# A hand-planned two-layer attention and MLP kernel: one row block's statistics moved to ScalarE, W2 loaded in two parts, and planner ranks set per step

## The chip, the cores and the metric

The kernel runs on one core of one Trainium2 chip. Its time is the device time of one execution in microseconds (us), as a median over several runs. A core has five engines with their own instruction streams: PE (TensorE, matmuls), DVE (VectorE), ACT (ScalarE), POOL (GpSimd) and SP (SyncE, which here only issues DMA transfers). PE reads SBUF and writes PSUM; ACT and DVE carry results from PSUM back to SBUF.

## The reference: two layers, each of windowed attention and an MLP

The input x has 2048 rows of 512 numbers in bf16. Weights are Wqkv (512 x 1536), Wo (512 x 512), W1 (512 x 1792) and W2 (1792 x 512), shared by both layers.

```python
for _ in range(2):
    x = x + attention(layernorm(x), wqkv, wo)   # 32 heads of 16, causal, window of 256 keys
    x = x + relu(layernorm(x) @ w1) @ w2
# attention: p = softmax(mask(q @ k.T * 16**-0.5)); o = p @ v; return concat(o) @ wo
# layernorm: (x - mean(x)) / sqrt(var(x) + 1e-5), no gain, no bias
```

## The kernel before: a planner writes each engine's order

The rows are cut into four chunks of 512. A step k is one chunk in one layer, so there are eight steps, 0 to 3 for the first layer and 4 to 7 for the second. In each step the work is:

- `plan_qkv(k)`: for each row block j of 128 rows (four in a chunk), statistics (`norm_stats`: `bn_stats` and `bn_aggr` on DVE, epsilon added for two blocks at once), the power -1/2 on POOL (`norm_pow`, for two blocks at once), the normalized bf16 block `xn` (`norm_apply`), and its transpose `xnT`. Step 0 transposes on PE with a copy out of PSUM, all others by a DMA transpose issued from SP. Then K, Q and V matmuls; `spread_k` writes K into the block-diagonal tile `KBD`, `spread_v` writes V into `V2f`.
- `plan_attention(k)`: scores, exp, masks and probabilities times V. Heads are handled in four tiles t of eight heads. A *score group* is a set of short matmuls `Sps<-Qt,KBD` into the one PSUM buffer `Sps` (four banks), followed by one exp on ACT (`Pb<-Sps`, up to 2048 elements per partition), followed by masks on `Pb` (`affine_select` on POOL or a minimum on DVE). There are 156 score groups, in a fixed order; group s may only start when the exp of group s-1 has read `Sps`. Below they are called S0 to S155, and the stretch from one to the next a *slot*. Then `acc<-V2f,Pb` (2880 matmuls of 34 columns, called pv below), a reciprocal and a multiply (`divide`) give O.
- `plan_rest(k)`: O is transposed (`OT<-O`, a DMA transpose from SP for each of the four row blocks, three buffers; on PE in the last step), multiplied by Wo, added to x; then the second layernorm (`xn`, `xn2T` again by DMA transposes), W1 with relu (`hT`, 14 groups of 4 matmuls) and W2 (4 groups of 14).

No order is written by hand. At build time each of these pieces is an `Op` with a key (its rank), the engines that may run it with a duration for each, and what it depends on. A list scheduler walks through time: when an engine is free it takes the ready Op with the lowest rank (on PE the key alone; on the others the ready time plus the key). The order that comes out is fixed in each engine's stream, so on the chip each engine runs its list in order and waits at each entry until its inputs are there. The ranks are `SOON` (for the copies out of PSUM, masks, divisions and additions), `calm` (statistics of early steps), `wait` (how many score groups ahead of its first use a K/Q group ranks, 16), the pace of V groups (1.6), and `d0`, `d1` (the stretch of score groups over which W1 and W2 are spread). `act_free` lets ACT take another piece ahead of the next exp only if that piece ends, by the planner's times, at most 0.1 us after the score group that is running, or 0.55 us after a coming one could start. When the planner sees PE idle for 0.4 us it inserts a matmul `warm<-ident` whose result nobody reads. Scores have the lowest key, so they go first; W1 and W2 fill what is left.

W2 is loaded by one DMA from SP, ranked after the transposes of step 1's `xnT`.

Of the kernel before, what the change touches and what calls it, by code (L numbers as in the profile page):

```python
# [15 lines left out]
P = 128  # L16
# [23 lines left out]
PW = 576  # L40
SHOW = None
# [29 lines left out]
def kernel(  # L71
# [122 lines left out]
    SOON = {'qkv': -0.5, 'v': 0, 'h': -1, 'mask': -1, 'div': 0, 'add': -2}  # L194
    LINK = {"PE": 0.2, "DVE": 0.2, "ACT": 0.2, "POOL": 0.2, "SP": 0.2}
# [64 lines left out]
    EVAC = {512: {"DVE": 0.67, "ACT": 0.59}, 256: {"DVE": 0.42, "ACT": 0.38}}  # L260
# [21 lines left out]
    def norm_stats(lid, j, src, deps, eps_from=None, key=0):  # L282
        def fn():
            st = small.tile([P, 6], FP32, name="st", bufs=4)
            dve.bn_stats(out=st[:], in_=src)
            dve.bn_aggr(out=mvs[:, lid % 8, j, :], in_=st[:])
            if eps_from is not None:
                dve.tensor_scalar_add(rstds[:, lid % 8, eps_from:j + 1], mvs[:, lid % 8, eps_from:j + 1, 1], 1e-5)
        return op(key, {"DVE": (0.86 + (0.18 if eps_from is not None else 0), fn)}, deps)

    def norm_pow(lid, j0, j1, deps, key=0):
        r = rstds[:, lid % 8, j0:j1]
        return op(key, {"POOL": (0.72, lambda: pool.tensor_tensor(out=r, in0=r, in1=mhalf[:, j0:j1], op=ALU.pow))}, deps)

    def norm_apply(lid, j, src, deps, by_array, dst, then_key, dst_deps):

        box = Box(xns)
        mv, r, nb = mvs[:, lid % 8, j, :], rstds[:, lid % 8, j:j + 1], nbs[:, lid % 8, j:j + 1]

        def fn(e):  # L300
            box.t = box.tile([P, D], BF16, "xn")
            if e == "DVE":
                dve.tensor_scalar(out=box.t[:], in0=src, scalar1=mv[:, 0:1], scalar2=r, op0=ALU.subtract, op1=ALU.mult)
            else:
                pool.tensor_tensor(out=nb, in0=mv[:, 0:1], in1=r, op=ALU.mult)
                pool.tensor_scalar(out=nb, in0=nb, scalar1=-1.0, scalar2=None, op0=ALU.mult)
                pool.tensor_scalar(out=box.t[:], in0=src, scalar1=r, scalar2=nb, op0=ALU.mult, op1=ALU.add)
        times = {"DVE": 0.52} if by_array else {"POOL": 1.4, "DVE": 0.54}
        a = op(-10 if lid == 0 else 0, options(times, fn), list(deps) + list(dst_deps), box)
        if by_array:  # L310
            return transpose(then_key, lambda: box.t[:], lambda: dst[0][:, :, j * P:(j + 1) * P], [a], [box])

        def dma():
            sp.dma_start_transpose(out=dst[0][:, :, j * P:(j + 1) * P],
                                   in_=box.t[:].rearrange("p (kc d) -> p kc d", kc=KC))
        return op(0, {"SP": (1.22, dma, 2.6)}, [a], None, [box])

    def transpose(key, src, dst, deps, uses, take=None):
        box = Box(psum)

        def fn():
            box.ps = box.tile([P, KC, P], BF16, "tp")
            for kc in range(KC):
                pe.transpose(box.ps[:, kc, :], src()[:, kc * P:(kc + 1) * P], ident[:])
        t = op(key, {"PE": (0.26, fn)}, deps, box, list(uses) + [box])
        return op(0, options({"DVE": 0.42, "ACT": 0.59}, lambda e: copy(e, dst(), box.ps[:])), [t], take, [box])
# [121 lines left out]
    c_tri = [op(3, {"POOL": (0.55, lambda i=i: triangle(i))}, [c_tri0]) for i in range(3)]  # L448
# [5 lines left out]
    c_v = [op(-2, {"DVE": (0.4, lambda e=e: v_ones(e))}, c_v0) for e in range(2)]  # L454
# [16 lines left out]
    def plan_qkv(k):  # L471
# [5 lines left out]
        calm = (-10, 1, 40, 60)[k] if k < 4 else 0  # L477
        for j in range(4):
            came = [d_x[j // 2] if c == 0 else d_xc[c]] if layer == 0 else [x_done[k - 4, j]]
            st.append(norm_stats(lid, j, src[j], came + applied.get(lid - 8, []), j - 1 if j % 2 else None, calm))  # L480
# [14 lines left out]
        wait = 0 if k == 0 else 16  # L495
        for h in range(2) if k == 0 else (None,):
# [5 lines left out]
            for t in range(4):  # L502
# [7 lines left out]
                k_done[k, t, h or 0] = op(SOON["qkv"], options(times, lambda e, t=t, h0=h0, h1=h1, box=box:  # L510
# [12 lines left out]
                q_done[k, t, h or 0] = op(SOON["qkv"], options(EVAC[w], qev), [m2], None, [box])  # L523
                mine += [m, m2]
        for j in range(4):
            at = first_slot[units_of[k][0]] + (1 + (8 if j > 1 else 0) if k == 0 else 1.6 * j - wait)
# [9 lines left out]
            ev = op(SOON["qkv"], options(EVAC[512], vev), [m], vs, [box, vs])  # L536
            v_done[k, j] = op(SOON["v"], options({"POOL": 1.72, "DVE": 1.42} if k else {"POOL": 1.72, "DVE": 1.42, "ACT": 1.48}, lambda e, j=j, vs=vs: spread_v(e, layer, c, j, vs.t[:])),
# [3 lines left out]
    def plan_attention(k):  # L541
        layer, c = divmod(k, NCH)
        prev = units_of.get(k - 1, []) if c else []
        for n in units_of[k]:
# [3 lines left out]
            for g in range(len(u.groups)):  # L548
# [17 lines left out]
                for m in u.masks(g):  # L566
                    times = {"DVE": 0.32 + 0.14 * (len(m) - 1), "POOL": 0.93 * len(m)}
                    masks[s].append(op(SOON["mask"], options(times, lambda e, m=m, g=g, pb=pb: mask(e, m, places(pb, g))), [exps[s]] + c_tri))
            for j0 in range(0, u.nq // 2, 2):
# [23 lines left out]
                def dfn(u=u, j=j, box=box):  # L593
# [4 lines left out]
                    SOON["div"], {"DVE": (0.64, dfn)}, [prior] + war + checks[k - 2:k - 1], None, [box])  # L598
# [3 lines left out]
    def plan_rest(k):  # L602
# [12 lines left out]
        for j in range(4):  # L615
# [6 lines left out]
            if final:  # L622
                t = transpose(-20000 + k, lambda j=j: O_of[k][:, j, :], to, ready, [ob], ob)
            else:
                t = op(-5, {"SP": (1.22, lambda j=j, to=to: sp.dma_start_transpose(
                    out=to(), in_=O_of[k][:, j, :].rearrange("p (kc d) -> p kc d", kc=KC)), 2.6)}, ready, ob, [ob])
# [8 lines left out]
            add = op(SOON["add"], {"DVE": (0.68, lambda j=j, box=box: residual(4 * c + j, box.ps[:], layer == 0))}, [m], None, [box])  # L635
# [11 lines left out]
        for j0, j1 in ((0, 2), (2, 4)) if k in HALVED else ((0, 4),):  # L647
            if k in HALVED:
                d0 = first_slot[units_of[k][3 + 2 * j0]] + 8
                d1 = d0 + 10  # L650
            else:
                d0, d1 = base[k + 1] + 7, base[k + 1] + 24
            n0, n1 = P * j0, P * j1
            evs = []
            for f in range(NF):
# [10 lines left out]
                evs.append(op(SOON["h"], options(EVAC[n1 - n0], hev), [m], None, [box]))  # L666
            for j in range(j0, j1):
                for n0, n1 in ((0, 256), (256, 512)) if final and j == 3 else ((0, 512),):
# [14 lines left out]
                    else:  # L683
                        x_done[k, j] = op(SOON["add"], {"DVE": (0.68, lambda j=j, box=box: residual(4 * c + j, box.ps[:], False))},
# [3 lines left out]
    for k in range(NSTEP):  # L688
        plan_attention(k)
        if k == 0:  # L690
            plan_qkv(1)
            d_w2 = op(0, {"SP": (1.4, lambda: sp.dma_start(w2[:], B_w2.rearrange("(f p) n -> p f n", p=P)), 9.0)}, applied[2])
        plan_rest(k)
        if 0 < k < NSTEP - 1:
            plan_qkv(k + 1)
# [50 lines left out]
    def act_free(t, us):  # L746
# [4 lines left out]
        if scores[s].number in started:  # L751
            return t + us <= score_end[0] + 0.1
        return t + us <= max(t, scores[s].at("PE")) + 0.55
# [22 lines left out]
    while events and events[0][0] < 3000:  # L776
# [16 lines left out]
        for e in ENGINES:  # L793
# [7 lines left out]
            elif e == "PE" and done_ops[0] < len(ops) - 12:  # L801
                if t - idle_since[0] >= (0.4 if t > 20 else 0.0) and sum(1 for f, _ in psum.free if f <= t) > 1:
# [167 lines left out]
```

## Time and profile before

| | |
|---|---|
| time, median of 9 runs | 481.33 us (480.7 to 483.81) |
| the profiled execution, own time | 482.59 us |
| its span, first to last instruction | 480.9 us |
| mean granted TensorE clock | 0.998 |
| busy: PE, DVE, ACT, POOL | 461.3, 356.1, 336.6, 300.0 us |
| `warm` matmuls | 40 |
| exps on ACT (`Pb<-Sps`), all forms | 156, 282.6 us, 1812 ns each |
| `OT<-O`, `xnT<-xn`, `xn2T<-xn` DMA transposes | 28 each, 2.5 us median from issue to landing |
| W1 and W2 loads | 1792 KB each, 11.1 us median to landing |

Busy time of PE is the union of matmul intervals, each counted from issue to the end of its pipeline; a busy PE can still be losing time. A row of the timeline gives the start, the length, the engine, the source line, the instruction, what it writes and reads, how many were merged, and in brackets how long the engine was idle before it and what ended that wait. All instructions of the step pieces go through one recording helper and so carry its line, L114; tiles are told apart by name. SPq rows are the issues of DMA transfers.

### The profile page before, as it was taken

Reading aid. Unit: us, or ns where it says so; the run is one execution under the profiler, and the core shown is the slowest. Engines: PE = TensorE matmul, PEld = TensorE weight load, DVE = VectorE, ACT = ScalarE, POOL = GpSimd, SP = SyncE. Lnnn points to the kernel's source line nnn. Section 1 sums busy time; section 2 is a strip of 40 time slices with the busy share of each in tenths; the row PEclk is TensorE's granted clock in tenths of the full one; section 3 lists DMA queues with packets and bytes.
Section 4 is the critical chain, followed back from the end, with each engine's and each line's share of the span. In section 5 each row is a group of like instructions: output and inputs, shape, how many; then the busy total and the mean of one; then the engine's idle time right before and its main releaser. Section 6 shows DMA issues by size and latency. Waiting matters only on the chain.

```text
span 480.9 us, 14303 instructions
## 1 busy us (share of the span) xinstructions
PE 461.3 (96%) x5967; PEld 244.3 (51%) x5967; DVE 356.1 (74%) x852; ACT 336.6 (70%) x263; POOL 300.0 (62%) x665
## 2 busy tenths in 40 slices
PE   7999999998999989999999999999999999999994
PEld 3555646654555535555544555544555545464443
DVE  6999988867987589977999887897559876464101
ACT  3878777877777668877778876777768777644330
POOL 7788868546776788846975766685766657421000
PEclk9999999999999999999999999999999999999999
DMA  8770321004200052002411023010331103000101
GB/s 266 254 204 3 68 23 25 2 3 67 57 12 3 2 90 45 4 1 45 68 24 36 12 34 57 12 35 2 56 68 25 34 1 68 25 1 11 34 12 38
DMA packets 54792, 21.96 MB, mean 46 GB/s; under 512 B 46145, under 2 KB 54209, under 8 KB 54721
## 3 DMA queue, kind: packets, MB, share of 16 engines
q1 hardware_dynamic: 54720, 20.98, 19.7%
q8 instruction: 48, 0.79, 0.7%
q14 instruction: 24, 0.19, 0.2%
HBM read 7.86 MB, written 2.10 MB: 21 GB/s over the span
## 4 chain that ended last, share of the span: by engine, by line
PE 80%; DMA 7%; POOL 6%; DVE 3%; issue 2%; ACT 1%; POOLq 0%; SPq 0%; ACTq 0%; DVEq 0%
PE ps_d L114 56%; PE acc L114 14%; PE Sps L114 9%; DMA OT<-O 4%; POOL Pb L114 3%; ACT Pb L114 1%; DMA xnT<-xn 1%; POOL xn L114 1%; POOL V2f L114 1%; POOL rstds L114 1%; DVE st L114 1%; DMA x_sb<-in_A_x_dram 1%; DMA xn2T<-xn 1%; POOL nbs L114 0%; DVE xn L114 0%
## 5 line engine op out<-in xcount | busy, mean ns | idle before, releaser
L114 ACT ACTIVATE Pb<-Sps 128x2048 bf16<-128x2048 f32 (+2 forms) x156 | 282.6, 1812 | 91.7 <-PE Sps L114 75.1
L114 POOL TENSOR_SCALAR_AFFINE_SELECT Pb<-Pb 64x256 bf16<-64x256 bf16 x498 | 219.4, 441 | 110.7 <-ACT Pb L114 90.7
L114 PE MATMUL ps_d<-xn2T,w 128*128 128x512 bf16 (+1 forms) x504 | 109.5, 356 | 0.5 <-DMA xn2T<-xn 0.5
L114 PE MATMUL ps_d<-w,hT 128*128 128x512 bf16 (+1 forms) x462 | 107.8, 373 | 0.0
L114 PEld LDWEIGHTS <-Pb 128*128 128x128 bf16 x2880 | 84.3, 96 | 26.4 <-issue 9.2
L114 PE MATMUL acc<-V2f,Pb 128*128 128x34 bf16 x2880 | 90.6, 178 | 2.2 <-POOL Pb L114 1.6
L114 DVE TENSOR_TENSOR Pb<-Pb,tri 128x512 bf16<-128x512 bf16 (+1 forms) x141 | 60.8, 436 | 16.4 <-ACT Pb L114 15.4
L114 PEld LDWEIGHTS <-w 128*128 128x128 bf16 x504 | 45.5, 97 | 44.6 <-issue 6.1
L114 PE MATMUL ps_d<-xnT,wqkv 128*128 128x512 bf16 (+1 forms) x288 | 66.4, 356 | 0.9 <-ACT KBD L114 0.9
L114 PEld LDWEIGHTS <-hT 128*128 128x128 bf16 x462 | 42.1, 98 | 45.7 <-issue 4.4
L114 PE MATMUL Sps<-Qt,KBD 32*128 32x320 bf16 (+3 forms) x1488 | 60.8, 251 | 1.2 <-ACT Pb L114 0.9
L114 DVE TENSOR_SCALAR hT<-ps_d 128x512 bf16<-128x512 f32 (+1 forms) x79 | 48.1, 619 | 16.3 <-PE ps_d L114 16.1
L114 PEld LDWEIGHTS <-KBD 32*128 32x128 bf16 x1488 | 23.4, 92 | 45.7 <-issue 42.5
L114 DVE TENSOR_SCALAR KBD<-ps_d,par 128x256 bf16<-128x256 f32 (+1 forms) x80 | 44.2, 601 | 0.9 <-PE ps_d L114 0.9
L114 DVE BATCH_NORM_STATS2 st<-x_sb 128x6 f32<-128x512 f32 (+1 forms) x64 | 43.7, 682 | 1.3 <-DMA x_sb<-in_A_x_dram 0.9
L114 DVE TENSOR_TENSOR x_sb<-ps_d,x_sb 128x512 f32<-128x512 f32 x48 | 32.4, 682 | 12.0 <-PE ps_d L114 11.9
L114 ACT ACTIVATE hT<-ps_d 128x512 bf16<-128x512 f32 (+1 forms) x47 | 26.2, 559 | 21.1 <-PE ps_d L114 21.1
L114 PEld LDWEIGHTS <-wqkv 128*128 128x128 bf16 x288 | 26.1, 97 | 25.6 <-issue 3.2
L114 PE MATMUL ps_d<-wo,OT 128*128 128x512 bf16 x128 | 32.9, 380 | 5.4 <-DMA OT<-O 5.2
L114 DVE TENSOR_TENSOR ob<-ps_d,x_sb 128x512 bf16<-128x512 f32 (+1 forms) x17 | 11.2, 660 | 34.6 <-PE ps_d L114 34.6
L114 POOL TENSOR_TENSOR rstds<-rstds,mhalf 128x2 f32<-128x2 f32 (+1 forms) x33 | 24.1, 731 | 16.7 <-DVE rstds L114 14.6
L114 PE MATMUL ps_d<-wqkv,xnT 128*128 128x512 bf16 x128 | 33.3, 380 | 0.0
(55 smaller groups left out, 279.9 us busy)
## 6 DMA issues: line engine op xcount, KB each, us to landing
w<-in_B_w_dram SPq DMA_DIRECT2D x2, 1792.0 KB, 11.1
out_dram<-ob SPq DMA_DIRECT2D x15, 128.0 KB, 1.7
wqkv<-in_A_wqkv_dram SPq DMA_DIRECT2D x3, 512.0 KB, 6.9
x_sb<-in_A_x_dram SPq DMA_DIRECT2D x3, 512.0 KB, 8.9
x_sb<-in_A_x_dram SPq DMA_DIRECT2D x2, 256.0 KB, 3.1
wo<-in_A_wo_dram SPq DMA_DIRECT2D x1, 512.0 KB, 8.9
xnT<-xn SPq DMA_TRANSPOSE x28, 2.5
OT<-O SPq DMA_TRANSPOSE x28, 2.5
```

The costliest lines, as they stand in the source:

```text
L114: inst = fn(*a, **k)
```

## The change

1. Statistics of row block 1 in step 0 move from DVE to ACT: `norm_stats_act` takes the mean with a Copy that accumulates and then the sum of squared distances with a Square whose bias is that mean. Epsilon is then added for blocks 0 and 1 one by one (`eps_op`).
2. W2 is loaded in two halves, with rank 3 instead of 0, the second after the first, and with 3.6 us of SP time each in the planner instead of 1.4.
3. Many planner constants become a table `TUNE`, looked up per step with `tune(name, k, value)`: the ranks of `SOON`, `calm`, `wait`, the pace of V, the stretch of W1 and W2, the slack of `act_free` (0.1 to 0.36 and 0.55 to 0.64), and the idle time before a `warm` matmul (0.4 to 0.72).
4. Durations that the planner believes are changed, among them a DMA transpose 2.6 to 2.9, a POOL mask 0.93 to 0.98, a division 0.64 to 0.72, `norm_apply` on POOL 1.4 to 1.58, statistics 0.86 to 0.91.

```diff
+TUNE = {
+    ("ones", 0): -5.34, ("tri", 0): 3.7, ("turn", 0): -5.56,
+    ("apply", 0): -7.11, ("apply", 1): -3.07, ("apply", 2): -4, ("apply", 3): -0.25, ("apply", 4): -2.96,
...
+    ("idle", 0): 0.72,
+    ("slack", 0): 0.64, ("slack", 1): 0.36,
+    ("qkv", 0): -1.86, ("qkv", 1): -1.27, ("qkv", 2): -2.62, ("qkv", 3): 0.04, ("qkv", 4): -0.59, ("qkv", 5): -0.15,
...
+    ("calm", 0): -3.34, ("calm", 1): 49.78, ("calm", 2): 53.98, ("calm", 3): 67.4,
+    ("wait", 1): 18.52, ("wait", 2): 19.8, ("wait", 3): 17.45, ("wait", 4): 14.78, ("wait", 5): 10.02,
+    ("wait", 6): 21.69, ("wait", 7): 18.69,
...
+    ("from", 1): 6.7, ("from", 2): 17.42, ("from", 3): 6.62, ("from", 4): -2, ("from", 5): 0.75, ("from", 6): 3.64,
+    ("from", 7): 13.08, ("from", (0, 0)): 12.46, ("from", (0, 2)): 16,
+    ("span", 1): 28.41, ("span", 2): 7.36, ("span", 3): 8.82, ("span", 4): 36, ("span", 5): 35.68, ("span", 6): 13.6,
+    ("span", 7): 25.51, ("span", (0, 0)): 13.4, ("span", (0, 2)): 21.1,
+}
+def tune(name, k, value):
+    return TUNE.get((name, k), value)
...
+    def norm_stats_act(lid, j, src, deps, key):
+        mv = mvs[:, lid % 8, j, :]
+        junk = Pb[1][:, 64:64 + D]
+        def fn():
+            act.activation(junk, src, ACT.Copy, scale=1.0 / D, accum_out=mv[:, 0:1])
+            act.activation(junk, src, ACT.Square, scale=-1.0, bias=mv[:, 0:1], accum_out=mv[:, 1:2])
+        return op(key, {"ACT": (1.4, fn)}, deps)
+    def eps_op(lid, j, by, deps, key):
+        return op(key, {"DVE": (0.18, lambda: dve.tensor_scalar(
+            out=rstds[:, lid % 8, j:j + 1], in0=mvs[:, lid % 8, j, 1:2], scalar1=by, scalar2=1e-5,
+            op0=ALU.mult, op1=ALU.add))}, deps)
...
-        return op(0, {"SP": (1.22, dma, 2.6)}, [a], None, [box])
+        return op(0, {"SP": (1.22, dma, 2.9)}, [a], None, [box])
...
+            if k == 0 and j < 2:
+                if j == 0:
+                    s0 = norm_stats(lid, j, src[j], came, None, calm)
+                    st.append(eps_op(lid, 0, 1.0, [s0], calm - 3))
+                else:
+                    s1 = norm_stats_act(lid, j, src[j], came, calm)
+                    st.append(eps_op(lid, 1, 1.0 / D, [s1], calm - 3))
+                continue
...
-        wait = 0 if k == 0 else 16
+        wait = 0 if k == 0 else tune("wait", k, 16)
...
-                d0, d1 = base[k + 1] + 7, base[k + 1] + 24
+                d0 = base[k + 1] + tune("from", k, 7)
+                d1 = d0 + tune("span", k, 17)
...
-            d_w2 = op(0, {"SP": (1.4, lambda: sp.dma_start(w2[:], B_w2.rearrange("(f p) n -> p f n", p=P)), 9.0)}, applied[2])
+            w2_in, d_w2 = B_w2.rearrange("(f p) n -> p f n", p=P), None
+            for f0, f1 in ((0, NF // 2), (NF // 2, NF)):
+                d_w2 = op(3, {"SP": (3.6, lambda f0=f0, f1=f1: sp.dma_start(w2[:, f0:f1, :], w2_in[:, f0:f1, :]), 5.0)},
+                          applied[2] + [d_w2])
...
-            return t + us <= score_end[0] + 0.1
-        return t + us <= max(t, scores[s].at("PE")) + 0.55
+            return t + us <= score_end[0] + tune("slack", 1, 0.1)
+        return t + us <= max(t, scores[s].at("PE")) + tune("slack", 0, 0.55)
...
-                if t - idle_since[0] >= (0.4 if t > 20 else 0.0) and sum(1 for f, _ in psum.free if f <= t) > 1:
+                if t - idle_since[0] >= (tune("idle", 0, 0.4) if t > 20 else 0.0) and sum(1 for f, _ in psum.free if f <= t) > 1:
```

The matmuls themselves, the tiles and the buffers are the same in both kernels; the two builds differ in the order of each engine's stream, in which of two engines runs some copies and masks, and in the number of `warm` matmuls.

## The prediction

> **What bounds the kernel now.** I read the page's busy table first, then the chain of waits, then PE's timeline.
>
> ```profile
> span 480.9 us, 14303 instructions
> PE 461.3 (96%) x5967; PEld 244.3 (51%) x5967; DVE 356.1 (74%) x852; ACT 336.6 (70%) x263; POOL 300.0 (62%) x665
> PE 80%; DMA 7%; POOL 6%; DVE 3%; issue 2%; ACT 1%; POOLq 0%; SPq 0%; ACTq 0%; DVEq 0%
> ```
>
> PE holds 80% of the chain that ended last; the next is DMA, 7%. A faster DVE or ACT alone brings nothing. The kernel ends sooner only if PE waits less or does less, so I keep a ledger of PE. Its prices come from the timeline:
>
> ```profile
> 152.06 1.52 PE L114 MATMUL acc<-V2f,Pb 128*128 128x34 bf16 x54
> ...
> 156.99 0.40 PE L114 MATMUL Sps<-Qt,KBD 32*128 32x320 bf16 x12
> 157.32 2.33 PE L114 MATMUL ps_d<-w,hT 128*128 128x512 bf16 x10
> 159.58 0.40 PE L114 MATMUL Sps<-Qt,KBD 32*128 32x64 bf16 x12
> ...
> 440.00 10.52 PE L114 MATMUL ps_d<-w,hT 128*128 128x512 bf16 x48
> ```
>
> Forty-eight matmuls of 512 columns take 10.52 us, of which the last one's pipeline is 0.38: (10.52 - 0.38) / 47 = 0.2157 us each. In the same way 0.0253 for one pv, and 0.109 for 256 columns (a row at 52.54 has twelve in 1.47). The middle rows are a regular slot: from one score group to the next 2.60 us, of which ten matmuls are 2.16 and 0.44 is the group with its fill and drain. I take 0.44 per slot as fixed; both kernels have 156 groups. A slot can't be shorter than its loop, group, exp, hand-over: about 0.62 plus the exp (1.88 for 2048 elements, so 2.50). The rest of a slot's time is loss. It sits at the ends of steps:
>
> ```profile
> 113.00 4.87 SPq L114 DMA_TRANSPOSE OT<-O  x3
> 113.23 0.81 PE L114 MATMUL warm<-ident 128*128 128x512 bf16 x3
> 114.58 0.82 PE L114 MATMUL warm<-ident 128*128 128x512 bf16 x3
> 117.91 1.27 SPq L114 DMA_TRANSPOSE xnT<-xn  x1
> 118.41 1.90 PE L114 MATMUL ps_d<-wo,OT 128*128 128x512 bf16 x8 [1.33 <-DMA OT<-O]
> 119.29 1.20 SPq L114 DMA_TRANSPOSE OT<-O  x1
> 121.75 1.04 PE L114 MATMUL ps_d<-wo,OT 128*128 128x512 bf16 x4 [0.57 <-DMA OT<-O]
> ...
> 172.31 1.21 SPq L114 DMA_TRANSPOSE OT<-O  x1
> 176.28 0.60 PE L114 MATMUL ps_d<-wo,OT 128*128 128x512 bf16 x2 [1.51 <-DMA OT<-O]
> ```
>
> The reader is to see that PE reaches the Wo matmuls before O's transpose has landed, that an xnT transpose stands between O's transposes in SP's queue, and that warm matmuls fill what the planner knew to be empty.
>
> Ledger of before (us; work = matmul counts from the built instruction order times the prices; loss = time - work - 0.44 per slot):
>
> S0-S20: time 43.16, work 31.19, loss 3.17
> S20-S40: 53.47, 42.71, 1.96
> S40-S60: 53.08, 40.99, 3.29
> S60-S80: 53.55, 42.93, 1.82
> S80-S155: 204.12, 169.07, 2.05
> Ahead of S0: 12.48, 6.94, 5.54. After S155: 61.04, 54.30, 6.74.
>
> Loss inside the slots is 12.29 (plus 20 warm matmuls, 4.3, counted as work).
>
> **The change, part by part.** I compared the two builds' instruction orders.
>
> *Work.* 36 warm matmuls instead of 40, all else equal: 4 x 0.2157 = -0.86. Of those after S0, before has 8 in S15-S17 and 12 in S40-S44; after has 16 between S7 and S11 and none later.
>
> *Head.* POOL's power for blocks 0 and 1 needs both statistics. Before it started at 6.26, on DVE's two statistics and epsilon (3.89 to 5.8). After, DVE does block 0, its epsilon, block 2, then block 1's epsilon, done about 6.1, and POOL has its memsets until 6.15 and now two triangle selects (0.55) ahead of the power: 6.7 to 7.4. ACT's two passes are not in the trace. The nearest rows are its 128x512 copy (0.60) and the same with a per-partition operand (0.68): 1.3, done by 5.3. If accumulating costs as much again, 2.6, done by 6.5, the power ends at 7.6; I take 1.3. Either way the first xn, behind a third statistic and two memsets in DVE's queue, comes at 7.85 (7.51 before). So the move gains nothing for the first xn; the fourth comes 0.6 earlier (9.4). But eight V and eleven K/Q matmuls now precede S0, and Q's copy follows K's two spreads on DVE: V at about 10.4 when its weights are there, K done 11.9, 0.87 + 0.42 on DVE, S0 at 13.3 (12.7 to 13.7 by when the weights land). Work ahead of S0 is 8.13, so loss 5.17: -0.37.
>
> *W2.* Issue 0.57 before, at 26.4; now two issues (0.57 to 1.87 each) behind the first two OT and all four xnT transposes, at about 40. Landing takes 11.1 median, 13.6 at most: there by 55; first use is after S28, past 76. Queued behind them on SP are the first two xn2T transposes, ready about 45 and used after S19, past 51: 1 to 3.7 late against 3 us of room. Zero; if that cover were gone, one for one.
>
> *S0-S20.* Step 1's statistics now rank last (`calm` 49.78), so its K/Q and V come after S12 instead of S8. Slot by slot, the larger of work + 0.44 and the loop gives 42.3, loss 4.17. Before, the same sum gave 42.67 against 43.16 measured; POOL's masks and V spreads feed pv here. I add 0.8: loss 4.97, 1.8 worse.
>
> *Step ends.* From the pv that completes O's first half to the first Wo matmul, the order leaves this PE time for steps 1 to 6: before 3.4, 4.5, 3.8, 4.3, 3.8, 3.8; after 4.2, 4.7, 4.5, 5.6, 4.7, 4.7. What is needed shows at 309.0 in the chain of waits: reciprocal 0.26, multiply 0.42, transpose 3.21, Wo at 313.05, so 4.0; at the chain's other lengths, 2.4 to 4.2, it is 3.2 to 5.0.
>
> ```profile
> 60.43 4.23 DMA OT<-O
> ...
> 309.79 3.21 DMA OT<-O
> ```
>
> In after, all four OT issues stand together in SP's queue at every step end; before, an xnT lay between them in steps 1 and 2, where the 12 warm matmuls and the longest waits are. Step 0's last two get 6.2 instead of 3.9. Where no xnT intervened (steps 3 to 6), before still lost 0, 0.54, 0.50 and 0.80 beyond the regular slot. I take 0.4 for seven ends, 2.8. The slot sum adds 1.13 where the loop is longer than the work. Loss from S20 on: 3.9, against 9.12.
>
> *Pause at S100.* Step 5's next K ranks behind W1 of step 3 (`wait` 10.02, `from` 6.62), so S101 comes after 13.7 us of other PE work. PE is fed, ACT idles; the work is missing later: after S155 there is 50.2 instead of 54.3. Zero.
>
> *Tail.* In step 7, between the second block's Wo and the first PE transpose of xn, before has 8 Wo and 33 other matmuls, after 8 and 19: 5.8 us. The chain add, statistics, power, normalize took from 430.46 to 435.9 before with two later statistics ahead of it on DVE; after has only one of them ahead, so about 4.7. Zero, with 1 us of cover.
>
> *ACT.* 13 more relu copies on ACT (47 to 60). The Trainium skill (ScalarE: Activation LUTs, Rules for kernel authors) wants relu on VectorE, as up to 3 times faster in bf16. The rows here, out of PSUM, say the reverse: 688 ns on DVE, 595 on ACT. By the rule ACT would take what DVE does in a third; by the rows DVE is relieved of 8.9 us and ACT given 7.7, both beside PE's work, so zero either way unless a copy delays an exp.
>
> *Fewer fillers.* The same skill (TensorE: Matmul & The Clock Gate, HAM oscillation) warns that PE gaps over about 3.4 us halve its clock; dropping the 12 at S40 could then cost about 1.7 us. But real work takes their place, the longest wait of a Wo row above is 1.51, and the granted clock is 0.998. I add nothing.
>
> **Sum.** Work -0.86, head -0.37, slots (4.97 + 3.9) - 12.29 = -3.4: -4.6. The profiled execution took 482.59 around its span of 480.9, so 478.0 by it; the median of 9 runs is 481.33, 1.26 lower, so 476.7. 0.3% (1.4 us) is about what a measurement of this kernel can tell from no change.
>
> **The rivals.**
> (a) Waits return, no change. Transposes land in 4.2 as at 60.4, since four xnT now stand right ahead of the four OT in step 1, and other pieces come late at new places; loss stays 12.3 and only the fillers and head count: 480.1. For it: 4.7 is under 5.0. Against: the row without an intervening xnT shows 3.21.
> (b) Late exps, slower. `act_free` now lets a copy end 0.36 after the score group instead of 0.1. The loop (2.50) has only 0.10 to spare in a regular slot, so an exp pushed back by more than 0.1 stretches the slot with PE idle. After has about 100 non-exp ACT pieces in the slots; 0.2 late each is 100 x 0.1 = +10, less 4.6: 486.7. It decides from 0.146 late on average. For: the widened slack. Against: ACT waits 0.72 for scores in a regular slot, more than a copy's 0.6.
> (c) All step-end waits vanish: another -2.8, and stage 0 as computed: 473.1.
> (d) The statistics' move doesn't do what it says: as worked out, the power starts later, not earlier, because POOL and DVE have other work queued ahead. That is inside the forecast.
>
> **How the numbers follow.** Forecast and (c) together 0.80 (0.62 and 0.18), (a) 0.12, (b) 0.08. Of (a), 0.03 falls to faster; faster 0.83, same 0.09, slower 0.08. The unknown costs (head 0.6, xn2T room 0.7, stage 0 1, ends 2.8) put the forecast's own range at 473 to 480; with rivals, 472.3 to 481.
>
> **What would show it.** Right: no warm matmul past 45 us; PE idle from DMA OT under 3 us (5.2 before); S155 near 419 with 50 us of work after it; S0 near 13.3; the power near 6.7. Wrong: PE waits at new places (POOL or ACT as releaser in S4-S12), regular slots over 2.65, or waits of PE for xn2T near 52.

## The result, and the profile after

The changed kernel takes 477.37 us (median of 10 runs, 476.24 to 478.58); beside it the kernel before took 481.85 (31 runs). The ratio is 0.9903, with a 95% interval of 0.9885 to 0.992: 4.5 us faster. The profiled execution took 475.28 us with a span of 473.6. That is 2.1 us under its kernel's own median and under every one of the ten runs, and this matters below.

The head of the page, then the answers on waits and on the chain, of the changed kernel:

```profile
span 473.6 us, 14312 instructions
PE 458.8 (97%) x5963; PEld 243.0 (51%) x5963; DVE 344.4 (73%) x833; ACT 346.9 (73%) x283; POOL 306.2 (65%) x679
PE 86%; DMA 4%; ACT 3%; DVE 2%; POOL 2%; issue 1%; SPq 0%; ACTq 0%; POOLq 0%
```

```profile
PE Sps L150 <- ACT Pb L150: 2.9, 8, 0.5
PEld L150 <- DMA OT<-O: 2.9, 4, 1.5
PE tp L150 <- DVE xn L150: 2.4, 1, 2.4
PE ps_d L150 <- DMA OT<-O: 1.8, 3, 1.0
```

PE's share of the chain rose from 80 to 86%, DMA's fell from 7 to 4%. PE waits 1.8 us for O's transpose (5.2 before), three times. The helper's line is now 150. Two waits are larger than before: the first PE transpose waits 2.4 us for xn (1.24), and scores wait 2.9 us for ScalarE's exps (0.9), seven of the eight times in S6 to S12.

The end of step 1, on the timeline (SP's queue and PE's Wo matmuls), where before an xnT stood between the third and fourth OT:

```profile
112.31 6.16 SPq L150 DMA_TRANSPOSE OT<-O  x4
115.61 0.38 PE L150 MATMUL ps_d<-wo,OT 128*128 128x512 bf16 x1
116.26 1.69 PE L150 MATMUL ps_d<-wo,OT 128*128 128x512 bf16 x7
119.21 0.60 PE L150 MATMUL ps_d<-wo,OT 128*128 128x512 bf16 x2 [1.05 <-DMA OT<-O]
```

All four OT transposes stand together and no filler is left here. One wait remains, and the chain says why: `DMA OT<-O` took 4.26 from 114.90 on, not 3.2.

The head, DVE, POOL and PE, on the timeline:

```profile
6.75 1.38 POOL L150 TENSOR_TENSOR rstds<-rstds,mhalf 128x2 f32<-128x2 f32 x2
7.60 0.33 DVE L150 MEMSET V2f<- 64x320 bf16 x1 [1.03 <-POOL rstds L150]
9.06 0.33 DVE L150 MEMSET V2f<- 64x320 bf16 x1 [1.14 <-issue]
9.42 1.38 DVE L150 TENSOR_SCALAR xn<-x_sb,mvs,rstds 128x512 bf16<-128x512 bf16 x4
9.89 0.40 PE L150 MATMUL tp<-ident,xn 128*128 128x128 bf16 x4 [2.44 <-DVE xn L150]
14.46 0.26 PE L150 MATMUL Sps<-Qt,KBD 32*128 32x192 bf16 x4
```

The power starts at 6.75, but the first xn only at 9.42 (7.51 before). Two fills of V2's ones columns stand ahead of it; each shows 0.33 busy and costs a gap of over 1 us besides. S0 is at 14.46 (12.48 before).

The prediction's ledger, filled in from the same execution (us; loss is time less counted work less 0.44 per slot):

```
                 predicted   before   after
Head loss           5.17      5.54     6.33
Loss S0-S20         4.97      3.17     3.85
Loss S20-S155       3.9       9.12     2.42
Tail loss           6.74      6.74     5.54
```

Work -0.86, head +0.79, slots 6.27 - 12.29 = -6.02, tail -1.20: together -7.3, which is the difference of the spans (480.9 to 473.6). The medians are 4.5 apart: the profiled execution of before lay 0.7 above its median here, that of the changed kernel 2.1 below. The gain in the slots does not hang on that one execution: the eight profiles with the changed kernel's order (this one and seven of the experiments) lose 1.6 to 3.8 in S20-S155, the kernel before 9.1.

### The profile page after: what moved, and what is told of

Same layout as the page of the kernel before. It is cut to its first block, busy times and chain, and to the rows that moved or that the text cites. A ratio compares the mean times of both kernels' runs of the same rounds, so it can differ in the third digit from the quotient of the medians.

```text
span 473.6 us, 14312 instructions
## 1 busy us (share of the span) xinstructions
PE 458.8 (97%) x5963; PEld 243.0 (51%) x5963; DVE 344.4 (73%) x833; ACT 346.9 (73%) x283; POOL 306.2 (65%) x679
## 4 chain that ended last, share of the span: by engine, by line
PE 86%; DMA 4%; ACT 3%; DVE 2%; POOL 2%; issue 1%; SPq 0%; ACTq 0%; POOLq 0%
PE ps_d L150 61%; PE acc L150 15%; PE Sps L150 10%; ACT Pb L150 3%; DMA OT<-O 3%; POOL Pb L150 1%; DVE st L150 1%; DMA xnT<-xn 1%; PE tp L150 1%; DMA x_sb<-in_A_x_dram 1%; DVE Pb L150 0%; DVE KBD L150 0%; POOL rstds L150 0%; POOL xn L150 0%; DVE xn L150 0%
## 5 line engine op out<-in xcount | busy, mean ns | idle before, releaser
L150 POOL TENSOR_SCALAR_AFFINE_SELECT Pb<-Pb 64x256 bf16<-64x256 bf16 x510 | 222.9, 437 | 102.6 <-ACT Pb L150 74.1
L150 PEld LDWEIGHTS <-Pb 128*128 128x128 bf16 x2880 | 82.6, 96 | 20.6 <-issue 8.2
L150 PE MATMUL acc<-V2f,Pb 128*128 128x34 bf16 x2880 | 88.2, 178 | 0.2
L150 DVE TENSOR_TENSOR Pb<-Pb,tri 128x512 bf16<-128x512 bf16 (+1 forms) x137 | 56.7, 423 | 12.9 <-ACT Pb L150 11.6
L150 DVE TENSOR_SCALAR hT<-ps_d 128x512 bf16<-128x512 f32 (+1 forms) x66 | 40.9, 624 | 17.8 <-PE ps_d L150 17.3
L150 DVE TENSOR_SCALAR KBD<-ps_d,par 128x256 bf16<-128x256 f32 (+1 forms) x86 | 46.5, 592 | 4.6 <-PE ps_d L150 4.4
L150 ACT ACTIVATE hT<-ps_d 128x512 bf16<-128x512 f32 (+1 forms) x60 | 33.0, 553 | 22.3 <-PE ps_d L150 21.5
```

Of the source, the lines that this page charges most:

```text
L150: inst = fn(*a, **k)
```

## Experiments

The theory: the gain is PE being fed at the step ends, and it takes both the ranks and the longer planned transpose; the statistics and the W2 parts bring nothing. Rivals: one of these parts brings it alone, or the clock has a hand in it. The other planned durations were not undone one by one. "Changed" stands for 477.37 us below; intervals are of ratios to the kernel before.

### Undoing the parts

**Statistics back on DVE**, the instruction order kept:

```diff
-            act.activation(junk, src, ACT.Copy, scale=1.0 / D, accum_out=mv[:, 0:1])
-            act.activation(junk, src, ACT.Square, scale=-1.0, bias=mv[:, 0:1], accum_out=mv[:, 1:2])
+            st = small.tile([P, 6], FP32, name="st", bufs=4)
+            dve.bn_stats(out=st[:], in_=src)
+            dve.bn_aggr(out=mv, in_=st[:])
...
-                    st.append(eps_op(lid, 1, 1.0 / D, [s1], calm - 3))
+                    st.append(eps_op(lid, 1, 1.0, [s1], calm - 3))
```

> The changed kernel in its own instruction order, with the second row block's statistics back on DVE (bn_stats, bn_aggr; 0.9 us) in place of ACT's two passes: the first part of the change undone alone. My theory (the statistics' move is worth nothing; the gain of 4.5 us sits at the step ends): DVE does one more statistics of 0.9 us ahead of its epsilon, so POOL's power starts 0 to 0.9 us later and S0 comes 0 to 0.9 later than the changed kernel's 14.46; time 477.4 to 478.3, the loss after S20 stays at 2.4. Rival 1 (the statistics on ScalarE bring the gain): time back at about 481.8. Rival 2 (ACT's passes were in the way of something): faster than 477.

478.71 us (0.9894 to 0.9954), the median of ten executions, one of which took 1483.79; without that one it is 478.51. The gain did not go with the statistics, so rival 1 falls. The first xn came at 10.22, S0 at 16.53, later than any theory said; the next kernel shows that most of that is not this edit. Against that kernel the first xn is 0.69 later and S0 0.29. So the move to ScalarE is worth 0.3 us at S0; the medians say 1.1 to 1.3, within intervals that overlap.

**W2 in one DMA**, order kept:

```diff
-                d_w2 = op(3, {"SP": (3.6, lambda f0=f0, f1=f1: sp.dma_start(w2[:, f0:f1, :], w2_in[:, f0:f1, :]), 5.0)},
+                d_w2 = op(3, {"SP": (3.6, lambda f0=f0: sp.dma_start(w2[:], w2_in) if f0 == 0 else None, 5.0)},
```

> The changed kernel in its own instruction order, with W2 loaded by one DMA of 1 MB at the first half's place and nothing at the second's: the second part of the change undone alone. My theory: the weights are used far later than they land either way, so 477.4 within 0.5, and PE's waits for OT in stage 0 and at the first step end (1.21 us of extra slot at 115) the same. Rival 1 (the split frees SP's queue or the DMA engines for the transposes): S0 to S20 loses 1 us or more beyond the 3.85 of the changed kernel, time 478.5 or more. Rival 2 (one issue in place of two gives SP 0.6 to 1.9 us back, so the xn2T transposes come earlier): 0.5 to 1 us faster.

477.31 us (0.988 to 0.9931): zero, as predicted. But its profile brought something new. Up to 20 us it has the changed kernel's instructions, and yet S0 is at 16.24 instead of 14.46. Busy time by window (columns: PE, PEld, DVE, ACT, POOL, granted clock, DMA share, GB/s), first the changed kernel, then this one:

```profile
8.00:10.00 2.00, 0.11 (x2) 0.12 (x3) 0.91 (x3) 0.00 (x0) 1.03 (x5) 1.00 1.07 364
10.00:12.00 2.00, 2.00 (x22) 1.42 (x21) 1.22 (x4) 1.45 (x3) 0.00 (x0) 1.00 1.09 359
12.00:14.00 2.00, 2.00 (x15) 1.27 (x13) 1.06 (x3) 1.62 (x4) 0.00 (x0) 1.00 1.11 350
```

```profile
8.00:10.00 2.00, 0.00 (x0) 0.00 (x1) 0.83 (x4) 0.00 (x0) 1.01 (x5) 1.00 1.07 369
10.00:12.00 2.00, 2.00 (x15) 1.44 (x16) 0.91 (x3) 1.19 (x2) 0.00 (x0) 0.55 1.10 362
12.00:14.00 2.00, 2.00 (x11) 1.01 (x9) 0.42 (x1) 0.60 (x1) 0.00 (x0) 0.59 1.10 348
```

PE does next to nothing from 8 to 10 in both. In one execution its clock is then 1.00, in the other 0.55 and 0.59: 22 matmuls from 10 to 12 become 15. PE's wait for the first xn was 2.44 and 2.07 us. Over all profiles of this study the wait and the clock behind it stand so:

```
wait under 0.5     clock 1.00   before with 2.9 or without late fillers, eight more fillers
wait 0.9 to 1.24   clock 1.00   before, and the kernels with the ones columns on ScalarE or POOL
wait 1.7           clock 1.00   no fillers after 20 us
wait 2.07          clock 0.55   W2 whole
wait 2.44, 2.5     clock 1.00   changed kernel, transpose planned at 2.6
wait 2.8 to 3.3    halved       no ranks, statistics on DVE, one rank of step 5
```

The length of the wait does not order the middle rows. The traces show what does. In all 14 profiles the stretches of half and of full clock, except those cut off by the ends of the trace, last 3.41 us or a whole multiple of it (half clock: 3.41 five times, 6.83 twice, 13.65 once). So the clock changes on a grid of 3.41 us, which lies differently in each execution. Two cells of it, first of the changed kernel, then of the kernel with W2 whole:

```profile
5.82:9.23 3.41, 1.62 (x8) 0.53 (x6) 1.17 (x5) 0.00 (x0) 3.06 (x9) 1.00 1.03 347
9.23:12.65 3.42, 2.76 (x27) 1.95 (x28) 1.96 (x6) 1.83 (x4) 0.00 (x0) 1.00 1.10 362
```

```profile
6.79:10.21 3.42, 1.35 (x9) 0.51 (x8) 1.33 (x5) 0.00 (x0) 2.22 (x6) 1.00 1.05 353
10.21:13.62 3.41, 3.41 (x21) 2.05 (x19) 1.13 (x4) 1.77 (x3) 0.00 (x0) 0.50 1.10 354
```

In the first, the wait falls into two cells, and PE is busy 1.62 us in the emptier one; in the second it lies in one cell with 1.35 us busy, and the next cell runs at half clock. Over all heads, behind the first fillers, the four cells with 1.1 to 1.35 us busy were followed by half clock, and none of the cells with 1.57 or more.

**All ranks undone**; statistics, W2 parts and new durations kept, the order built anew:

```diff
-TUNE = {
-    ("ones", 0): -5.34,
...
-}
+TUNE = {}
```

> The changed kernel with its table of ranks emptied, so every step has the ranks of the kernel before, with the statistics on ScalarE, the two W2 parts and the new durations kept: the order is built anew and has 45 warm matmuls (36 in the changed kernel), 15 of them at the ends of the first two steps. My theory (the ranks bring the gain): the built order alone asks for a loss of 10.7 us in the slots, so PE waits as before at the step ends and the fillers are back; 481 to 487. Rival (the durations, or statistics and W2 parts, bring the gain and the ranks only ride along): 476.5 to 478.5.

483.73 us (1.0022 to 1.0051): 6.4 us above the changed kernel and slower than before. The ranks are needed. Not as I had put it, though: PE's wait for OT is 1.3 us in this profile. The fillers at the step ends are back (45 in all), stage 0 loses 6.5 us in S0-S20 (3.85), S20-S155 loses 5.0 (2.42), and the granted clock is 0.76 and 0.82 in the windows 8 to 12 and 12 to 16, and 0.74 and 0.83 from 32 to 40.

**Only the planned transpose**, on the kernel before:

```diff
-        return op(0, {"SP": (1.22, dma, 2.6)}, [a], None, [box])
+        return op(0, {"SP": (1.22, dma, 2.9)}, [a], None, [box])
...
-                    out=to(), in_=O_of[k][:, j, :].rearrange("p (kc d) -> p kc d", kc=KC)), 2.6)}, ready, ob, [ob])
+                    out=to(), in_=O_of[k][:, j, :].rearrange("p (kc d) -> p kc d", kc=KC)), 2.9)}, ready, ob, [ob])
```

> The kernel before with one of the change's edits: a DMA transpose is planned at 2.9 us in place of 2.6; statistics, W2 and ranks as before. The order built from that has 43 warm matmuls (40 before), and from O's first half to the first Wo matmul it leaves 3.8, 4.2, 4.7, 4.9, 4.5, 4.2 us (before 3.4, 4.5, 3.8, 4.3, 3.8, 3.8; changed kernel 4.2 to 5.6); step 1 still has an xnT between O's transposes. My theory (planned room for the transposes takes away the waits at the step ends, the ranks give the real work to put there): PE's wait for OT falls from 5.2 to 2 to 3 us but fillers stand in its place, so 480.3 to 481.8, less than half of the change's gain. Rival (the planned durations alone bring the gain): 477 to 479. Rival 2 (no gain without the ranks): 481.8 or more.

479.57 us (0.9953 to 0.9975): 1.9 us, less than half of the gain, from one number; PE's wait for OT fell further than I expected, to 1.2 us. At the end of step 2 the timeline shows it work, SP's queue and Wo, first of the kernel before, then of this one:

```profile
170.99 1.21 SPq L114 DMA_TRANSPOSE xnT<-xn  x1
172.21 0.60 PE L114 MATMUL ps_d<-wo,OT 128*128 128x512 bf16 x2
172.31 1.21 SPq L114 DMA_TRANSPOSE OT<-O  x1
...
176.28 0.60 PE L114 MATMUL ps_d<-wo,OT 128*128 128x512 bf16 x2 [1.51 <-DMA OT<-O]
```

```profile
169.32 0.81 PE L114 MATMUL ps_d<-wo,OT 128*128 128x512 bf16 x3
169.75 6.81 SPq L114 DMA_TRANSPOSE xnT<-xn  x4
170.39 0.39 PE L114 MATMUL ps_d<-wo,OT 128*128 128x512 bf16 x1
171.70 1.03 PE L114 MATMUL ps_d<-wo,OT 128*128 128x512 bf16 x4
```

The xnT no longer stands ahead of the last OT, and the loss of S60-S80 goes from 1.82 to 0.04. The queue is only a part of the 1.51, though: that OT also took 3.93 us from issue to landing, where 2.5 is the median; with 2.9 it took 2.42. In the kernel before without its late fillers (below) the same xnT stands ahead of the same OT, which took 2.49, and PE did not wait for it. At the end of step 1, where an xnT still stands between, S40-S60 keeps 2.73 of its 3.29; of PE's two waits there, 0.88 is for a transpose of 3.94 us ahead of the xnT and 0.31 for the one behind it.

**The counterpart**: the changed kernel with 2.6 again in the same two lines.

> The changed kernel with one edit undone: a DMA transpose is planned at 2.6 us again; ranks, statistics and W2 stay. It is the counterpart of the kernel before with 2.9 (479.6). The order built from it has the same 36 warm matmuls, and from O's first half to the first Wo matmul it leaves 5.1, 4.0, 4.5, 4.0, 4.3, 4.0 us (4.2 to 5.6 with 2.9); its slots ask for 1.8 us more by their own work and loop. Theory (4.0 is what a transpose at 3.2 needs, so some waits come back beside the 1.8): PE's wait for OT 3 to 5 us in the profile (1.8 in the changed kernel), median 479 to 481. Rival (the ranks carry the gain whatever the planned duration): 477.0 to 478.5.

481.29 us (0.997 to 1.0016): 3.9 us of the gain gone, a little more than expected. With all ranks in place, the planner's shorter transpose brings an xnT back between two OTs, at the end of step 5, and only there. It is not what PE waits for:

```profile
327.04 5.13 SPq L150 DMA_TRANSPOSE OT<-O  x3
...
332.39 1.19 SPq L150 DMA_TRANSPOSE xnT<-xn  x1
332.84 1.04 PE L150 MATMUL ps_d<-wo,OT 128*128 128x512 bf16 x4 [1.49 <-DMA OT<-O]
333.67 1.22 SPq L150 DMA_TRANSPOSE OT<-O  x1
334.07 1.04 PE L150 MATMUL ps_d<-wo,OT 128*128 128x512 bf16 x4 [0.19 <-DMA OT<-O]
```

The wait of 1.49 us ends with the second OT, issued at 328.28 and 4.52 us on its way, the next one with the third, 4.40 us on its way; both were issued ahead of the xnT, and for the fourth, behind it, PE did not wait. This order leaves 4.3 us from O's first half to the first Wo matmul here, 4.7 with 2.9: too little room for slow transposes is what shows, not the xnT. That slot alone loses 2.02 us; PE's wait for OT is 3.0 us in all. S20-S40 loses 2.93 instead of 0.36: the order's own slots ask for 1.2 of that, and the chain shows an xnT transpose of 4.00 at 61.21. So ranks without the duration bring 0.5 us (not told from zero), the duration without the ranks 1.9, both 4.5. They don't add up: each order is built as a whole.

### The head

**Ones columns filled on POOL**:

```diff
-        dve.memset(V2[64 * e:64 * e + 64, :, e, :, 16:17], 1.0)
+        pool.memset(V2[64 * e:64 * e + 64, :, e, :, 16:17], 1.0)
```

> The changed kernel in its own instruction order, with the two fills of V2's ones columns on POOL in place of DVE. In the changed kernel each of them holds DVE for 0.33 us and a gap of 1.03 to 1.14 us besides, ahead of all four normalizations. Theory (these two, 2.7 us together, hold back the first xn, which the prediction mis-sized as 0.33 each): first xn 1.5 to 2.7 us earlier than 9.42, S0 at 12.0 to 13.3 instead of 14.46, time lower by 1 to 2.5, so 475 to 476.4. Rival (something else is late next: the weights' landing or POOL's own queue, with the power at 6.75 behind the fills or V's spreads pushed back): S0 stays within 0.5 of 14.46 or a later slot gives the gain back, time 477.4 within 0.5.

476.67 us (0.9867 to 0.992). The first xn came at 7.46, nearly 2 us earlier. But each fill took POOL 1.46 us, and the first stands between the two powers; the normalizations beside it slowed to 0.9 us each on DVE (0.35). S0 at 14.97: the rival was right in the profile, and the time is within the interval of the changed kernel.

**Eight more fillers ahead of the first transpose**:

```diff
+                    warms[0] += 1
+                    def warmup(box=box, n=9 if warms[0] == 17 else 1):
+                        ps = box.tile([P, 512], FP32, "warm")
+                        for _ in range(n):
+                            mm(ps[:], ident[:], ident[:].rearrange("p (o q) -> p o q", o=1).to_broadcast([P, 4, P]), True, True)
+                    d.opts = {"PE": (d.opts["PE"][0], warmup)}
```

> The changed kernel with eight more filler matmuls (1.7 us at the full clock) behind the seventeenth, where PE waits 2.1 to 2.4 us for the first xn; nothing else differs. The kernel with W2 whole, whose instructions up to 20 us are those of the changed kernel, showed a granted clock of 0.55 and 0.59 at 10 to 14 us after that wait and S0 at 16.24, where the changed kernel's profile showed 1.00 and S0 at 14.46. Theory (in most executions of the changed kernel the clock halves after that wait and costs 1.8 us): the clock stays at 1.00 there, S0 near 14.5 in the profile, median 475.3 to 476.2. Rival 1 (the clock in the head is no part of the difference between medians and the profiled run): 477.4 within 0.5. Rival 2 (the fillers end too late and hold back the transposes): S0 later by up to 0.8.

475.87 us (0.9846 to 0.9894), S0 at 14.46 and the clock at 1.00. Work that computes nothing took 1.5 us off the median (five executions; the intervals overlap by a little). The theory holds in part. The mean granted clock of each execution is on record: with W2 whole, half clock in the head went with a mean of 0.995. Of twelve executions of the changed kernel five have 0.994 or 0.995 and take 478.1 on average, seven have 0.997 or more and take 476.7; with the eight fillers all five have 0.997 or more. If those five are the ones with a half clock in the head, it comes in under half of the executions, for about 1.4 us each. The rest is not the clock: this profile, with the changed kernel's S0 and a clock of 1.00 up to its last 1.4 us, has a span of 476.0 against 473.6, lost a little at a time from S0 on.

**Ones columns on ScalarE**:

```diff
-        dve.memset(V2[64 * e:64 * e + 64, :, e, :, 16:17], 1.0)
+        act.copy(V2[64 * e:64 * e + 64, :, e, :, 16:17],
+                 ones_bf[64 * e:64 * e + 64, 0:16].rearrange("p (o a q) -> p o a q", o=1, q=1).to_broadcast([64, NSLOT, 16, 1]))
```

> The changed kernel in its own order with the two fills of V2's ones columns as copies on ScalarE, which stands idle from 5.2 to 10.3 us, in place of DVE (and not on POOL, where they took 1.46 us each, stood between the two powers and slowed DVE's normalizations from 0.35 to 0.9 us). Theory: first xn at about 7.5, PE's wait ahead of the first transpose under 1 us so that the clock holds; then the weights (landed at about 10.3) and DVE's spreads set S0: 12.7 to 13.5, as the prediction had it for two short fills (13.3). S0 is 1.0 to 1.8 earlier than in the profile of the changed kernel and the half clock is gone: median 473.6 to 475.3. Rival (the head is not worth its whole length, since stage 0 then waits for POOL's V spreads, masks and xnT): S0 early, loss from S0 to S20 up by as much, 476.5 to 477.4.

475.26 us (0.9839 to 0.9888): the lowest median of the study, and below both kernels (ahead of the changed one by 2.1 us, the intervals just touching). PE's wait is 0.91, the clock holds. S0 came at 13.92, later than expected, and the timeline names the next two in line:

```profile
6.18 3.15 ACT L150 COPY V2f<-ones_bf 64x320 bf16<-64x320 bf16 x2 [1.12 <-POOL V2f L150]
9.36 1.67 ACT L150 ACTIVATE xnT<-tp 128x512 bf16<-128x512 bf16 x3
10.89 1.04 PE L150 MATMUL ps_d<-wqkv,xnT 128*128 128x512 bf16 x4 [0.50 <-DMA wqkv<-in_A_wqkv_dram]
```

The fills cost as much on ScalarE and hold back its copies of xnT; and right behind, K's weights land at 10.9.

**Only 8 of 20 slots at first**, the others behind step 1's first power:

```diff
+        ones_fill(act.copy, e, 0, 8)
...
+            if lid == 2 and j0 == 0:
+                for e in range(2):
+                    ones_fill(act.copy, e, 8, NSLOT)
```

> The changed kernel with the ones columns filled on ScalarE, but at first only for the 8 of 20 slots that step 0 reads; the other 12 follow on ScalarE behind step 1's first power. The whole fills took 1.4 to 1.6 us each on DVE, POOL and ScalarE alike, that is 4.3 to 4.9 ns for each of 320 scattered elements. Theory (the price goes by the element, and ScalarE's 3.15 us held back the copies of xnT): 0.55 to 0.65 us each for the first two, ScalarE free at about 7.4, fourth xnT transposed by 9.3, first K matmul set by its weights' landing alone (10.3 to 10.9), S0 at 13.3 to 13.9, and the clock at 1.00; median 474.6 to 475.5 (the kernel with whole fills on ScalarE: 475.26). Rival 1 (the price is fixed per instruction): 1.4 us each again, S0 at 13.9, 475.3. Rival 2 (the later fills, 1 us each, get in the way of exps near step 1's start): 476 or more.

476.92 us (0.9868 to 0.9909), no better. The first fills took 0.74 us each for 128 elements, the later ones 1.03 for 192: with 1.58 for 320 that is 4.3 to 4.5 ns for each further element. ScalarE was free early, but K's weights landed at 11.20, so S0 came at 14.24; and rival 2 happened, the later fills at 21.27 delaying a V copy that PE then waited 1.5 us for.

### Fillers and the pause

**The kernel before without its 20 fillers after the head**:

```diff
-                    d.opts = {"PE": (d.opts["PE"][0], lambda box=box: mm(
+                    d.opts = {"PE": (d.opts["PE"][0], lambda box=box, t=t: t < 20 and mm(
```

> The kernel before without its 20 filler matmuls after the head (8 around the end of step 0, 12 around the end of step 1): the part 'fewer fillers' of the change alone. The prediction's claim (they lie in waiting time, so dropping them costs nothing and brings nothing): 481.8 within 0.6. Rival 1 (the 0.86 that the prediction credits for four fillers fewer holds: they delay work behind them by their 0.2157 us each): up to 4.3 lower, 477.5 to 480.5. Rival 2 (the clock gate: without them PE's waits at the two step ends grow to 2 to 4 us and the clock halves for 3.4 us or so each): a granted clock near 0.5 at about 60 or 113 to 120 us, 483 to 485.

483.01 us (1.0005 to 1.0035): 1.5 us slower without them. Its windows show the reason (PE's clock is the third figure from the end):

```profile
52.00:56.00 4.00, 3.81 (x25) 2.36 (x26) 3.39 (x10) 2.60 (x3) 3.70 (x7) 0.50 0.21 37
116.00:120.00 4.00, 3.32 (x22) 1.01 (x19) 1.92 (x8) 2.50 (x2) 3.00 (x8) 0.50 0.52 100
```

No single wait was over 1.2 us here, yet PE was busy only 2.34 and 2.77 of the 4 us ahead (48 to 52 and 112 to 116). The profile's S20 is 2.13 later than before, of which 0.8 is won back; the second stretch adds about 0.5.

**The changed kernel without its 16 fillers after the head**, the same edit.

> The changed kernel in its own order without its 16 filler matmuls between S7 and S11. In the kernel before, dropping the 20 after the head brought back two stretches of half clock (at 50 to 59 and 114 to 123 us) and cost 1.5 us. Theory (fillers are worth the clock that they hold, not their own time): PE's gaps of up to 1.1 us in S7 to S11 grow, no single one reaches 2 us, yet the share of idle time in a stretch of 3 to 4 us comes to a third; if the clock halves, it is at 28 to 36 us and costs 1 to 2: 478 to 479.5. Rival 1 (gaps under 2 us never halve the clock): 477.4 within 0.5. Rival 2 (the fillers delayed real work): faster by 0.5 to 1.5.

475.61 us (0.983 to 0.988), faster than the changed kernel by 1.8, against my theory. The clock did halve, and longer than anywhere else:

```profile
28.00:32.00 4.00, 2.18 (x52) 1.80 (x56) 3.43 (x11) 2.81 (x2) 2.69 (x7) 0.50 0.00 0
32.00:36.00 4.00, 1.42 (x40) 0.94 (x31) 3.55 (x12) 2.90 (x2) 3.50 (x8) 0.50 0.18 35
36.00:40.00 4.00, 4.00 (x80) 2.40 (x80) 3.10 (x9) 2.31 (x2) 2.29 (x5) 0.50 0.68 71
```

The half clock lasts 13.65 us. From 28 to 36 DVE is busy 3.4 to 3.6 of 4 us and PE 1.4 to 2.2 at half clock: PE isn't the bound there, and S0-S20 took only 1.2 us more than in the changed kernel's profile. The two profiled spans are level (474.0 and 473.6), but the changed kernel's is that of its lowest time, and this one's of a time near the top of its five. Where the 1.8 us of the medians come from, perhaps from the head's clock (1.00 in this profile, PE's wait 1.7), no run settles.

**Step 5's rank set back to 16**:

```diff
-    ("wait", 1): 18.52, ("wait", 2): 19.8, ("wait", 3): 17.45, ("wait", 4): 14.78, ("wait", 5): 10.02,
+    ("wait", 1): 18.52, ("wait", 2): 19.8, ("wait", 3): 17.45, ("wait", 4): 14.78, ("wait", 5): 16,
```

> The changed kernel with one rank set back: step 5's K and Q may start 16 slots ahead (before: 16; changed kernel: 10.02). The order built from it cuts the pause between S100 and S101 from 13.7 us of other work to a few us; the 5.2 us of work that are missing there then come after S155 (55.4 instead of 50.2). Prediction's claim (PE is fed in the pause, so it costs zero): 477.4 within 1, with the slots' own sum 0.7 worse. Rival 1 (the pause costs what ScalarE loses in it, part of its 8.7 idle us): 1 to 4 us faster. Rival 2 (the shorter tail is the gain, because the tail loses more per us of work): 479 or more.

478.01 us (0.9884 to 0.9931), level with the changed kernel: the pause costs nothing that can be measured. S96-S116 loses 0.7 less without it, S116-S136 1.8 more (PE's longest wait there, 1.10 us at 322.29, is for DVE's spread of K).

## Why the prediction was right, and where it was not

The sum (-4.6) met the medians (-4.5), and that they met so closely is luck. In the profiles from which it was worked out the parts come to -7.3: the slots brought 2.6 more than forecast, the tail 1.2 more, the head 1.2 less. The medians lie 2.8 closer together than these two executions, and that made up for it. The direction and the place of the gain were right for the reason given, PE fed at the step ends.

- **Step ends: right in kind, too cautious.** Fillers past 45 us are gone, PE's wait for OT is 1.8 (under 3 was asked for), S155 is at 417.86 (near 419) with 50.2 us of work behind it. The terms: 0.4 for each of seven ends and 1.13 from the slot sum made 3.9; measured 2.42. Stage 0's 4.97 was 3.85: the 0.8 added for late masks and spreads did not come. That slots in S20-S155 carry the gain is shown by the ledger; that it takes the planned transpose and the ranks together, by the kernels with 2.9 alone, 2.6 again and no ranks. One reading was wrong: that the xnT between two OTs made the longest waits. At the end of step 1 the 1.33 us ended with the OT issued at 114.30, ahead of that xnT (117.91); it took 4.06 us to land. Only the 0.57 behind it was for an OT behind the xnT, and the 1.51 of step 2 is in part. Transposes of about 4 us came in every profile, with an xnT near or not (the changed kernel: 4.26 among four OTs in a row); of the 42 waits of PE for OT in the 14 profiles, 39 ended with one that took 3.2 us or more. What the change brings is room for them: 4.2 to 5.6 us instead of 3.4 to 4.5. No run changed that room alone, so how much of the 6.7 us in these slots is owed to it is not shown; PE's waits for OT make up 3.4 of them.
- **Head: wrong.** "First xn at 7.85" failed, and with it S0 at 13.3. The power did start at 6.75 (6.7), ScalarE's statistics were done at 5.16 (5.3). The step that failed counted "two memsets" at their busy 0.33 each. Each costs 1.36 to 1.47 with the gap ahead of it, which the trace of before showed as a gap of 1.17 in front of its second fill. That is 2.2 us more of DVE's time; the first xn came 1.57 and S0 1.16 later than predicted. With both fills off DVE the first xn starts at 7.46.
- **"Fewer fillers: I add nothing": wrong for the head.** I weighed the rule of the Trainium skill (TensorE: Matmul & The Clock Gate, HAM oscillation: no PE gaps over about 3.4 us) only at S40 and found the longest Wo wait, 1.51, well under it. At S40 that held. In the head the change makes a wait of 1.7 to 3.3 (five profiles with its head), and in two of them half clock followed: 1.8 us at S0. The same page (What's actually happening) says that the activity window runs free of the kernel's start, which fits the clock halving after 2.07 us in one execution and not after 2.44 in another, as the cells above show; the measured waits replace its 3.4 as a bound. The kernel before is not free of it: of its 93 executions beside the experiments, 25 have a mean clock under 0.996 and take 1.8 us more than the others, though its profile shows 1.00 up to the end; at which place is not on record.
- **Profile against median.** I took the executions' offset (1.26) from before. The changed kernel's profiled execution lies 2.1 under its median instead of above it. The half clock in the head may account for a part of this, about 1.4 us in five of twelve executions; the rest stays open.
- **Tail: not zero.** Loss 5.54 instead of 6.74. PE's part is as long as counted; the 1.2 lies behind the last addition, 4.5 us to the span's end against 5.7, part of it the last output's issue (0.35 against 0.72). Six other profiles with the changed kernel's order show 5.53 to 5.59 (a seventh 6.2); with the order of before, 6.82 (with 2.9) and 6.4 (without late fillers). Part goes by the execution: the last output took 2.65 us to land before and 1.69 after, but 2.68 in that seventh and 1.73 without late fillers. The rest stays open.
- **W2, pause, ReLU on ScalarE: zero, as said.** W2 and the pause by their kernels. Scores wait 2.0 us more for exps than before, nearly all in S6 to S12: PE waiting for ACT in S4 to S12 is a sign that the prediction named as being wrong. It stayed inside the size allowed: these slots hold only 0.7 to 1.7 us of work, less than their loops of 1.4 and 2.3 us (0.62 and exps of 0.81 and 1.66), which the slot sum had counted, and S0-S20 loses 3.85 of the 4.97 forecast. Beyond S20 such a wait came once (0.39), so rival (b) did not come.
- **Rival (d)** held as worked out: the statistics' move does not start the power earlier. Undone, it costs 0.3 us at S0.

## What to carry to other kernels

Give a transfer room by its slow landings, not by its median: the transposes' median was 2.5 us, PE waited for those of 3.2 to 4.6, and one planned duration, 2.9 for 2.6, brought 1.9 us alone. One more transfer ahead in the queue, at 1.2 us, takes from the same room. Cost a wait of PE by the clock behind it too: fillers in a gap of 2 us can be worth their place, where PE is the bound afterwards. Compare medians before explaining a difference of two profiles: here the profiles were 7.3 us apart and the medians 4.5. And take an instruction's price from the start of one to the start of the next, with the idle time in brackets, not from its busy time alone.

## What was not expected of the hardware

- A fill of 64 partitions by 320 single elements of two bytes took 1.36 to 1.47 us on DVE (of which the record shows 0.33), 1.46 on POOL and 1.58 on ScalarE, where each further element took 4.3 to 4.5 ns (128, 192 and 320 elements).
- PE's clock halved after waits of 2.07 to 3.3 us, not after 1.24, and in between it differed from execution to execution: it changes on a grid of 3.41 us, and what told in the heads was whether one cell had under 1.4 us of PE's work or over 1.5. It halved also without such a wait, where short matmuls kept PE busy 2.3 and 2.8 of 4 us.
- Of the 84 DMA transposes in each profile, 15 to 24 took over 3 us to land, at a median of 2.5; no run shows why.
- An accumulating pass on ScalarE issues a second instruction: `ACTIVATION_READ_ACCUMULATOR`, 0.19 us.
- While POOL filled, DVE's normalizations took 0.9 us instead of 0.35.
